# Last 512 queries in two halves, B's x loads behind the read of x's staging tile, six VectorE score banks in groups 3, 7 and 11

## Chip, cores, metric

One core of a Trainium2 chip runs the whole program. The metric is device time in microseconds of an execution. A run is called fast or slow by its state; slow runs are left out of every comparison. Ratios are computed as the mean time of one kernel's fast runs over the mean of the other's fast runs of the same rounds, so they are not quite the ratio of the medians quoted beside them.

## The reference

Two attention blocks over 2048 positions of width 448, 16 heads of 28, bf16. A has one key and value head that all query heads share, and full softmax over all 2048 keys. B looks back over 8 positions, two apart.

```python
def _A_ref(x, wq, wk, wv, wo):
    q = (x @ wq).reshape(B, S, H, Dh).transpose(0, 2, 1, 3)
    k = x @ wk; v = x @ wv                         # one head
    p = softmax(einsum("bhqd,bkd->bhqk", q, k) * Dh ** -0.5)
    return einsum("bhqk,bkd->bhqd", p, v) ... @ wo
def _B_ref(x, wqkv, wo):                           # window 8, dilation 2
    ...
return concatenate([a, b], axis=-1)
```

## The kernel before

A Python list scheduler lays out the order of all instructions on PE (TensorE), ACT (ScalarE), DVE (VectorE), POOL (GpSimd) and SP (SyncE) when the program is built, from estimated durations (below, `pr` is an operation's priority, lower first, and `rel` the earliest time for it in the list's own clock, in us); on the chip each engine runs its list in that fixed order. So a changed estimate, priority or dependence can reorder everything after it.

A's scores: a *quad* is 512 queries x 4 heads, 16 quads in all (group q below is quad q). Each quad has 64 score banks of 128 keys x 512 queries. ScalarE exponentiates three or two banks at a time; VectorE takes one of the three in some rounds.

```python
SLOTS = ((0, 1, 2), (3, 4))      # PSUM banks of the two score slots
PVBANK = 5; XBANKS = (6, 7)      # P.V sums; everything else
TAILB = (0, 1, 2, 4); WARM = 7
OFF_AT = {q: (0, 2, 5, 7) for q in range(1, 16)}             # rounds with a bank on VectorE
OFF_AT.update({q: (0, 2, 3, 5, 7, 8) for q in (5, 9, 13)})
```

The loads. x of A's first 512 rows goes to a staging tile (`xst`), the other chunks and B's x come by DMA transposes, all from one queue in the order of `pr`; A's chunks 1 to 3 (`pr=-20 + c`) wait for the staging tile, B's x (`pr=-16 + c`) doesn't wait.

```python
for c in range(1, NCH):      # A's chunks 1 to 3 wait for the staging tile
    ... e.dma_start(out=g.xT_A[...], transpose=True), R=["xst"], W=[("xT", c, t)], pr=-20 + c)
for c in range(NCH):         # B's x: no wait
    ... e.dma_start(out=g.xT_B[...], transpose=True), W=[("xT_B", c, t)], pr=-16 + c)
a("sp", ...  B's q and k weights ..., pr=-16.5, rel=4)
a("gp", ...  B's V weights (wqv) ..., pr=-7)
# ... wo_B, wo4 ..., pr=2
a("sp", ... e.dma_start(out=g.v_dram[0:PAD, :], in_=g.Vst[0:PAD, 0, :]),   # zero rows before V
  R=[("Vst", 0)], W=[("vd", -1)], dsem="i_vz", land=2.5, pr=3, rel=4)
```

B's V of each block of 128 rows is copied by VectorE from PSUM to `Vst[:, k % 2]` and stored to a scratch in HBM. The zero rows are stored *from* `Vst[:, 0]` too, so the first V copy has to wait until that store has read them.

The end of the last quad, cut:

```python
for hf in range(2 if last else 1):       # evacuation of P.V in halves, all after the last P.V
    ... transpose, reciprocal, tensor_tensor, transpose
for s4 in range(4):                      # four blocks of 128 queries
    u = Use(..., (TAILB[s4],), late=True) if last else Use(..., XBANKS)
    ... four output matmuls, one copy (VectorE, or ScalarE if last and s4 is odd), one store
```

Of the kernel before, what the change touches and what calls it, by code (L numbers as in the profile page):

```python
# [29 lines left out]
XBANKS = (6, 7)  # L30
TAILB = (0, 1, 2, 4)
WARM = 7
QT = 27.0
# [5 lines left out]
OFF_AT = {q: (0, 2, 5, 7) for q in range(1, 16)}  # L39
OFF_AT.update({q: (0, 2, 3, 5, 7, 8) for q in (5, 9, 13)})  # L40
LATE = 2
# [52 lines left out]
class Sched:  # L94
# [49 lines left out]
    def run(self, engines):  # L144
# [44 lines left out]
        while left:  # L189
# [77 lines left out]
            if e == "pe":  # L267
                if o.use is not None and o.use.spare and o.alone and area(T) < (self.WANT if limit is None or T + o.dur + 0.18 <= limit + self.EPS else self.LOW):
                    o.fill = 1
                    o.dur += 0.18  # L270
                    o.dense += 512 - o.use.spare
                elif (o.full and area(T) < (self.FULL[o.full] if T + 0.22 * o.full + 0.2 <= H + self.EPS else self.LOW)
                      and all(d.start is not None and d.end + self.lat(d) <= T for d in o.opt)):
                    o.deps.update(o.opt)
                    o.dur = 0.22 * o.full
                    o.tiled = False
                    o.dense = 512 * o.full
                elif o.fill is not None:
                    o.full = 0
                    o.fill = max(0, min(0 if waiting else 2, round((self.WANT - area(T)) * self.WIN / 512 + 0.3)))  # L280
                    if T > 14 and area(T) > self.LOW:
                        o.fill = max(0, min(o.fill, int((H - 0.12 - self.MODE - T - o.dur + self.EPS) / 0.22)))
                    o.dur += 0.22 * o.fill
                    o.dense += 512 * o.fill
                if o.tiled and not mode:
                    o.dur += self.MODE
                mode = o.tiled
                if o.dense:
                    recent.append((T + o.dur, o.dense))
                    del recent[:-120]  # L290
# [108 lines left out]
class Gen:  # L399
# [185 lines left out]
    def loads(self):  # L585
# [20 lines left out]
        for c in range(NCH):  # L606
            for t in range(4):
                a("sp", 1.05, one(lambda e, c=c, t=t: e.dma_start(
                    out=g.xT_B[:, t, 512 * c:512 * c + 512], in_=g.B_x[0, 512 * c:512 * c + 512, XB0[t]:XB0[t] + 128],
                    transpose=True)), W=[("xT_B", c, t)], dsem=f"i_xb{c}.{t}", land=4.5, pr=-16 + c)  # L610
        a("sp", 1.2, lambda e: [
# [113 lines left out]
    def a_q(self, sc, first=False):  # L725
# [3 lines left out]
        for t in range(4):  # L729
# [16 lines left out]
            else:  # L746
# [11 lines left out]
              R=["qadd"], W=[("qT", par, t)], use=u, pr=pr if first else -1)  # L758

    def a_loop(self):  # L760
        g, a = self, self.s.add
        units = [(sc, t, tb, j) for sc in range(4) for t in range(4) for tb in range(16) for j in range(4)]
        assert len(units) == NU
        g.last_exp, g.pvs, g.evacs = {}, {}, []
        quads = {(sc, t): [[] for _ in range(4)] for sc in range(4) for t in range(4)}
        dqs = {k: [[] for _ in range(4)] for k in quads}
# [5 lines left out]
        while pos < NU:  # L772
# [9 lines left out]
            def qk(e, us=us, b0=b0, box=[]):  # L782
                for _ in range(box[0].fill):
                    e.matmul(g.bank(b0), g.warm[:, 0:128], g.warm[:, :], start=True, stop=True)
                for i, (sc, t, tb, j) in enumerate(us):
                    if box[0].full:
                        r = e.matmul(g.bank(b0 + i), g.kz[:, j, 128 * tb:128 * tb + 128], g.qT[:, sc % 2, t, :], start=True, stop=True)  # L787
                        continue
                    r = e.matmul(g.bank(b0 + i), g.kT[32 * j:32 * j + 32, 128 * tb:128 * tb + 128],  # L789
                                 g.qT[32 * j:32 * j + 32, sc % 2, t, :], start=True, stop=True, tile_position=(32 * j, 0))  # L790
                return r
            box = []
            o = a("pe", 0.315, lambda e, qk=qk, box=box: qk(e, box=box), R=[("kT", tb // 4) for (_, _, tb, _) in us] + [("qT", sc % 2, t) for (sc, t, _, _) in us],
                  W=[("ring", slot)], pr=-50)
            box.append(o)
            o.ring = o.tiled = True
            o.full = len(us) if len(us) > 1 else 0
            o.opt = {x for (_, _, tb, _) in us for x in g.kz_ops[tb // 4]}
            o.fill = 0
# [10 lines left out]
            for i in range(na):  # L810
                g.last_exp[b0 + i] = x
                quads[us[i][:2]][us[i][3]].append((us[i], ("expT", n % ERING), g.expT[:, n % ERING, 512 * i:512 * i + 512], 0))
            if off:
# [4 lines left out]
            while late and late[0][0] <= n // 2:  # L818
                for x in late.pop(0)[1]:
                    qd = x[0][:2]  # L820
                    g.nq[qd] = g.nq.get(qd, 0) + 1
# [9 lines left out]
            for u in us:  # L831
                js = quads[u[:2]]
                while all(js):
                    g.pv_group([x.pop(0) for x in js])
                if u[2:] == (15, 3):
                    left = [x.pop(0) for x in js if x]
# [3 lines left out]
    def pv_group(self, grp):  # L840
        g, a = self, self.s.add
        qd = grp[0][0][:2]
        all_pv = g.pvs.setdefault(qd, [])
        box = []

        def pv(e):
            for (_, _, tb, j), _, src, w in grp:
                order = [o.seq for o, js in all_pv if j in js]
                first, last = box[0].seq == min(order), box[0].seq == max(order)
                x = e.matmul(g.bank(PVBANK, p0=32 * j, p1=32 * j + 32), g.v_aug[:, w, tb, :], src,  # L850
                             start=first, stop=last, tile_position=(0, 32 * j))
            return x
        o = a("pe", 0.315, pv, R=sorted({y[1] for y in grp}) + sorted(
            {(k, y[3], y[0][2] // 4) for k in ("v_aug", "v_aug1") for y in grp}), pr=-40, dense=700)
        o.tiled = o.pv = True
# [5 lines left out]
        g.npv[qd] = g.npv.get(qd, 0) + len(grp)  # L861
        if g.npv[qd] == 64:
            g.a_quad_end(*qd)

    def offload(self, n, us):

        g = self
        if n % 2 or us[0][:2] != us[-1][:2]:
            return 0
        if us[0][:2] != g.quad:  # L870
            g.quad, g.round = us[0][:2], n // 2
        return int(n // 2 - g.round in OFF_AT.get(4 * us[0][0] + us[0][1], ()))

# [26 lines left out]

    def a_quad_end(self, sc, t):
        g, a = self, self.s.add
        end = 12.0 + QT * (4 * sc + t + 1)
        last = sc == 3 and t == 3
        evacs = []
        hv = 2 if last else 1
        for hf in range(hv):
            w, b = 512 // hv, 16 // hv
            cs, bs = slice(w * hf, w * hf + w), slice(b * hf, b * hf + b)
            keys = [hf] if last else [0, 1]  # L910
            kk = lambda n: [(n, t % 2, x) for x in keys]
            p0 = -30 if last else -1
            o = a("dve", t_dve_ps(w), lambda e, cs=cs: e.transpose(out=g.PV_T[:, t % 2, cs], in_=g.bank(PVBANK)[:, cs]),  # L913
                  W=kk("PV"), pr=-30)
            o.deps.update(x for x, _ in g.pvs[sc, t])
            evacs.append(o)
            pt = g.PV_T[:, t % 2, :].rearrange("p (b e) -> p b e", e=32)
            a("dve", 0.25, lambda e, pt=pt, bs=bs: e.reciprocal(out=g.rden[:, t % 2, bs], in_=pt[:, bs, DH]),
              R=kk("PV"), W=kk("rden"), pr=p0)
            a("dve", t_dve_1x(w), lambda e, pt=pt, bs=bs: e.tensor_tensor(  # L920
                out=g.oN[:, bs, :], in0=pt[:, bs, :], in1=g.rden[:, t % 2, bs].unsqueeze(2).to_broadcast([128, b, 32]), op=ALU.mult),
              R=kk("PV") + kk("rden"), W=[("oN", x) for x in keys], pr=p0)
            a("dve", 0.12 + 1.04e-3 * w, lambda e, cs=cs: e.transpose(
                out=g.oTn[:, t, cs], in_=g.oN[:, :, :].rearrange("p b e -> p (b e)")[:, cs]),
              R=[("oN", x) for x in keys], W=[("oTn", t, x) for x in keys], pr=p0)
        g.evacs = evacs
        pr = end + 20
        if t < 3:
            return
        for s4 in range(4):  # L930
            blk = 4 * sc + s4
            if last:
                u = Use(f"F{sc}.{s4}", (TAILB[s4],), late=True)
            else:
                u = Use(f"F{sc}.{s4}", XBANKS)
            for tt in range(4):
                o = a("pe", t_mm(D), lambda e, u=u, s4=s4, tt=tt: e.matmul(  # L937
                    g.bank(u.bank, D), g.oTn[:, tt, 128 * s4:128 * s4 + 128], g.wo4[:, tt, :], start=tt == 0, stop=tt == 3),
                  R=[("oTn", tt, s4 // 2), "wo4"], W=[u], use=u, pr=pr + s4 + tt if not last else -30 + tt, dense=448)
                if last and tt == 0:  # L940
                    o.deps.add(g.last_exp[TAILB[s4]])
            ob = blk % 4
# [63 lines left out]
    def b_logits(self, k):  # L1006
# [4 lines left out]
        for t in range(4):  # L1011
# [9 lines left out]
            if k == 0:  # L1021
                op.deps.update(g.s.rd.get("xst", ()))
        u = Use(f"L{k}", XBANKS, spare=128)
# [114 lines left out]
```

## Time and profile before

| | before |
|---|---|
| median | 461.12 us, 461.11 over the six runs of the comparison |
| first exponential starts / last ends | 11.29 / 451.72 us |
| span of the profile | 459.19 us |
| head, stream, tail | 11.29, 440.43, 7.47 us |
| TensorE clock | 1.000 |

"Stream" is from the start of ScalarE's first score exponential to the end of the last, "tail" from there to the end of the span. In a row of a profile stand the start and the duration in us (chain, timeline), or busy us and mean ns of one (groups); what follows in brackets or behind the last bar is the idle time of the engine before it and what ended it. PEld is PE's weight load.

### The profile page before, as it was taken

What the parts mean: (1) busy time and instruction counts of PE and PEld (TensorE: products, weight loads), DVE (VectorE), ACT (ScalarE), POOL (GpSimd) and SP (SyncE); (2) the same over time, 40 slices, a digit from 0 to 9 for tenths busy, and PEclk for the clock granted to TensorE, in tenths of its full rate; (3) what the DMA queues carried; (4) which work ended last, traced back from release to release, by engine and by line L of the source; (5) the groups of instructions that cost most, each with busy time, mean ns of one, the idle gap of its engine ahead of it and who ended that gap; (6) DMA issues with size and microseconds to landing.
All of it is one profiled execution on the core that took longest, in us unless ns stands there. A gap on an engine that the chain in (4) does not pass through costs nothing.

```text
span 459.2 us, 8717 instructions
## 1 busy us (share of the span) xinstructions
PE 427.7 (93%) x3682; PEld 163.6 (36%) x3682; DVE 380.7 (83%) x622; ACT 444.9 (97%) x430; POOL 9.4 (2%) x29
## 2 busy tenths in 40 slices
PE   8999999999999989999899999899899998989997
PEld 3333232323533324234353342224244342325343
DVE  6556889988798898989688889998988969889883
ACT  3999999999999999999999999999999999999994
POOL 7000000000000000000000000000000000000000
PEclk9999999999999999999999999999999999999999
DMA  7774303002201002020220120002022221214001
GB/s 152 128 162 95 109 27 100 1 1 90 92 15 40 19 10 82 20 81 22 81 91 30 44 83 18 0 13 92 0 97 92 70 78 30 72 31 142 10 1 61
DMA packets 42102, 27.34 MB, mean 60 GB/s; under 512 B 17474, under 2 KB 41904, under 8 KB 42064
## 3 DMA queue, kind: packets, MB, share of 16 engines
q1 hardware_dynamic: 40464, 25.28, 19.6%
q0 software_dynamic: 304, 0.73, 0.6%
q10 hardware_dynamic: 1296, 0.79, 0.5%
q8 instruction: 29, 0.48, 0.4%
q14 instruction: 9, 0.07, 0.1%
HBM read 17.60 MB, written 5.52 MB: 50 GB/s over the span
## 4 chain that ended last, share of the span: by engine, by line
ACT 86%; PE 11%; DVE 1%; DMA 1%; issue 0%
ACT expT L806 85%; PE ps L789 2%; PE ps L1079 2%; PE ps L850 2%; PE ps L787 1%; DMA stage<-in_A_x_dram 1%; PE ps L978 1%; PE ps L1086 1%; PE ps L937 1%; ACT e_t L1054 0%; PE ps L654 0%; PE ps L738 0%; PE ps L1028 0%; PE ps L434 0%; PE ps L993 0%
## 5 line engine op out<-in xcount | busy, mean ns | idle before, releaser
L806 ACT ACTIVATE expT<-ps 128x1024 bf16<-128x1024 f32 (+1 forms) x410 | 438.8, 1209 | 2.1 <-PE ps L789 1.9
L789 PE MATMUL ps<-qT,kT 32*128 32x512 bf16 x824 | 122.3, 385 | 11.6 <-ACT expT L806 9.3
L850 PE MATMUL ps<-expT,v_aug 128*32 128x512 bf16 x958 | 94.8, 389 | 1.0 <-ACT expT L806 1.0
L787 PE MATMUL ps<-qT,kz 128*128 128x512 bf16 x200 | 59.6, 383 | 9.9 <-ACT expT L806 9.4
L789 PEld LDWEIGHTS ps<-qT,kT 32*128 32x128 bf16 x824 | 30.1, 91 | 91.7 <-ACT expT L806 68.4
L883 DVE TENSOR_SCALAR d_x<-ps 128x512 f32<-128x512 f32 x66 | 45.4, 688 | 17.9 <-PE ps L789 16.8
L850 PEld LDWEIGHTS ps<-expT,v_aug 128*32 128x32 bf16 x958 | 24.3, 93 | 62.0 <-issue 55.4
L1073 DVE TENSOR_TENSOR prod<-Vsh,a_n 128x896 bf16<-128x896 bf16 x64 | 37.5, 614 | 7.9 <-PE ps L1079 7.9
L1019 DVE TENSOR_TENSOR stage<-qTB,kTB 112x1024 bf16<-112x1024 bf16 x64 | 42.3, 674 | 1.8 <-PE ps L1028 1.7
L1079 PE MATMUL ps<-ident,prod 128*112 128x128 bf16 x512 | 41.8, 224 | 0.0
L894 DVE SCALAR_TENSOR_TENSOR d_u<-d_u,d_x 128x1024 f32<-128x1024 f32 x33 | 40.1, 1215 | 0.1
L896 DVE SCALAR_TENSOR_TENSOR dexp<-d_u,d_x 128x1024 int16<-128x1024 f32 x33 | 40.0, 1213 | 0.1
L892 DVE SCALAR_TENSOR_TENSOR d_u<-d_x 128x1024 f32<-128x1024 uint16 x33 | 39.9, 1209 | 0.2
L1079 PEld LDWEIGHTS ps<-ident,prod 128*112 128x112 bf16 x512 | 34.2, 130 | 14.7 <-issue 10.9
L978 PE MATMUL ps<-xT_B,wqkv 128*128 128x512 bf16 x128 | 38.9, 383 | 0.0
L787 PEld LDWEIGHTS ps<-qT,kz 128*128 128x128 bf16 x200 | 12.2, 97 | 31.1 <-ACT expT L806 28.9
L1028 PEld LDWEIGHTS ps<-ones,stage 112*128 112x128 bf16 x512 | 18.5, 96 | 7.8 <-issue 4.8
L1028 PE MATMUL ps<-ones,stage 112*128 112x4 bf16 x512 | 21.2, 167 | 0.0
L738 PE MATMUL ps<-xT_A,wq 128*128 128x512 bf16 x64 | 19.8, 384 | 0.1
L1086 PE MATMUL ps<-wo_B,oT 112*128 112x448 bf16 x64 | 18.1, 357 | 0.0
L993 PE MATMUL ps<-wqv,xT_B 128*128 128x448 bf16 x64 | 17.5, 356 | 0.0
L913 DVE STREAM_TRANSPOSE PV_T<-ps 128x512 f32<-128x512 f32 (+1 forms) x17 | 11.4, 676 | 6.7 <-PE ps L850 6.5
(103 smaller groups left out, 303.3 us busy)
## 6 DMA issues: line engine op xcount, KB each, us to landing
Vsh<-v_scratch SPq DMA_DIRECT2D x16, 896.0 KB, 4.6
v_scratch<-Vst SPq DMA_DIRECT2D x16, 112.0 KB, 1.7
out_dram<-outB SPq DMA_DIRECT2D x16, 112.0 KB, 1.7
out_dram<-outA SPq DMA_DIRECT2D x14, 112.0 KB, 1.7
wqkv<-in_B_wqkv_dram SPq DMA_DIRECT2D x1, 672.0 KB, 5.4
stage<-in_A_x_dram ACTq DMA_DIRECT2D x1, 448.0 KB, 4.0
wo_B<-in_B_wo_dram SPq DMA_DIRECT2D x4, 98.0 KB
wo<-in_A_wo_dram SPq DMA_DIRECT2D x4, 98.0 KB
```

The source lines that it names most:

```text
L787: r = e.matmul(g.bank(b0 + i), g.kz[:, j, 128 * tb:128 * tb + 128], g.qT[:, sc % 2, t, :], start=True, stop=True)
L789: r = e.matmul(g.bank(b0 + i), g.kT[32 * j:32 * j + 32, 128 * tb:128 * tb + 128], g.qT[32 * j:32 * j + 32, sc % 2, t, :], start=True, stop ...
L806: x = a("act", t_exp(w), lambda e, b0=b0, w=w, n=n: e.activation(g.expT[:, n % ERING, 0:w], g.ps[:, 512 * b0:512 * b0 + w], ACT.Exp, scale ...
L850: x = e.matmul(g.bank(PVBANK, p0=32 * j, p1=32 * j + 32), g.v_aug[:, w, tb, :], src, start=first, stop=last, tile_position=(0, 32 * j))
L883: o = a("dve", t_dve_ps(512), lambda e: e.tensor_scalar(out=xx[:, 512 * h:512 * h + 512], in0=g.bank(bank), scalar1=-128.0 * A2, scalar2=1 ...
L892: a("dve", t_dve_1x(1024), lambda e: e.scalar_tensor_tensor(out=u, in0=lo, scalar=EP * F, in1=lo, op0=ALU.add, op1=ALU.mult), R=di, W=["d_ ...
L894: a("dve", t_dve_1x(1024), lambda e: e.scalar_tensor_tensor(out=v, in0=u, scalar=EQ * F * F, in1=lo, op0=ALU.add, op1=ALU.mult), R=["d_u"] ...
L896: a("dve", t_dve_1x(1024), lambda e: e.scalar_tensor_tensor(out=out, in0=v, scalar=EL / F ** 3, in1=xx, op0=ALU.mult, op1=ALU.subtract), R ...
L978: a("pe", t_mm(512), lambda e, u=u, t=t, kt=kt, w=w: e.matmul(g.bank(u.bank), g.wqkv[:, kt, w * D + KC * t:w * D + KC * t + 128], g.xT_B[: ...
L1019: op = a("dve", t_dve_2x(1024), lambda e, t=t, qv=qv, kv=kv: e.tensor_tensor(out=g.prodT[0:KC, t, :, :], in0=qv, in1=kv, op=ALU.mult), R=R ...
L1028: r = e.matmul(g.bank(u.bank, 128).rearrange("p (h w) -> p h w", w=WIN)[:, 4 * t:4 * t + 4, w], g.prodT[0:KC, t, w, :], g.ones4[:, :], sta ...
L1079: a("pe", 0.056, lambda e, u=u, t=t, w=w: e.matmul(g.bank(u.bank, 128, 128 * t, p1=KC), g.prod2[:, w, KC * t:KC * t + KC], g.ident[:, :], ...
```

## The change

Its intent: split the last quad so that half of it is finished before the stream ends; keep B's transposes from going ahead of A's; let B's first products wait only for PE's reads of the staging tile; take VectorE's extra banks earlier.

```diff
-TAILB = (0, 1, 2, 4)
-WARM = 7
+TAILB = (4, 0)
+WARM = 9
-OFF_AT.update({q: (0, 2, 3, 5, 7, 8) for q in (5, 9, 13)})
+OFF_AT.update({q: (0, 2, 3, 5, 7, 8) for q in (3, 7, 11)})
+OFF_AT[15] = (0, 2, 3, 5)
@@ the scheduler's estimate after filler matmuls
-                if o.tiled and not mode:
+                if o.tiled and (not mode or o.fill):
@@ B's x loads
-                    transpose=True)), W=[("xT_B", c, t)], ...
+                    transpose=True)), R=["xst"], W=[("xT_B", c, t)], ...
@@ the last quad's units: 2 x 128 keys by 256 queries, first half of the queries first
+    def parts(self, u):
+        if u[:2] == (3, 3):
+            return [(2 * (u[2] % 8) + i, 256 * (u[2] // 8), 256) for i in range(2)]
+        return [(u[2], 0, 512)]
@@ scores and P.V: one matmul for each part; P.V sorted by parts
@@ evacuation and output of each half on its own (cut)
-        for s4 in range(4):
+        for s4 in range(4) if hf is None else (2 * hf, 2 * hf + 1):
@@ B's first products
-                op.deps.update(g.s.rd.get("xst", ()))
+                op.deps.update(o for o in g.s.rd.get("xst", ()) if o.eng == "pe")
```

## The prediction

> **What bounds the kernel now.** I read the page first: busy shares, the chain that ended last, the costliest groups. Then the chain in order of time, first over the whole span and then over its last 7 us; then the timeline of the head and of the last quad, a "quad" being the work for 512 queries by 4 heads.
>
> ```profile
> PE 427.7 (93%) x3682; PEld 163.6 (36%) x3682; DVE 380.7 (83%) x622; ACT 444.9 (97%) x430; POOL 9.4 (2%) x29
> ACT 86%; PE 11%; DVE 1%; DMA 1%; issue 0%
> L806 ACT ACTIVATE expT<-ps 128x1024 bf16<-128x1024 f32 (+1 forms) x410 | 438.8, 1209 | 2.1 <-PE ps L789 1.9
> L883 DVE TENSOR_SCALAR d_x<-ps 128x512 f32<-128x512 f32 x66 | 45.4, 688 | 17.9 <-PE ps L789 16.8
> ```
>
> The first line gives each engine's busy time, the second the chain's shares by engine. ScalarE's exponentials (line 806) are the chain. The first starts at 11.29 us and the last ends at 451.72, and in those 440.4 us ScalarE sat idle for 2 us at most. The span of 459.2 us is therefore a head of 11.3, a stream of 440.4 and a tail of 7.5. VectorE computes the exponential for 66 of the 1024 score banks (the last line's x66).
>
> The rows by form say what the stream is made of:
>
> ```profile
> L806 ACT ACTIVATE expT<-ps 128x1024 bf16<-128x1024 f32 x270 | 269.7, 1066 | 0.1
> L806 ACT ACTIVATE expT<-ps 128x1536 bf16<-128x1536 f32 x139 | 207.2, 1490 | 2.0 <-PE ps L789 1.9
> L1054 ACT ACTIVATE e_t<-lg 128x256 f32<-128x256 f32 x8 | 3.5, 434 | 0.0
> ```
>
> The fastest start-to-start distance in the timeline is 0.903 us for a 1024-wide one and 1.33 us for a 1536-wide one. Thus 270 x 0.903 + 139 x 1.33 = 428.7 us is the floor of the exponentials; the other exponentials of line 1054 add eight times about 0.3 = 2.5, the four small ones of the head 0.6 and the last 512-wide one 0.8. The remaining 7.8 us are many small waits for scores, spread evenly.
>
> The tail, as the chain has it:
>
> ```profile
> 452.03 0.36 PE ps L850 x4
> 452.38 0.02 issue
> 452.41 0.78 DVE PV_T L913 x2
> 453.19 0.24 DVE rden L918 x2
> 453.43 0.64 DVE oN L920 x2
> 454.07 0.36 DVE oTn L923
> 454.43 0.05 issue
> 454.48 0.75 PE ps L937 x3
> ...
> 455.78 0.60 DVE outA L947
> 456.39 0.59 DVE outB L1089
> ```
>
> After the last P.V matmuls, VectorE evacuates, normalises and transposes 512 queries, as two interleaved halves (x2); PE makes the output products, VectorE copies two blocks and then B's last block, and the store takes the rest, 456.98 to 459.2 = 2.2 us.
>
> **What the Trainium skill says.** (1) "ScalarE: Activation LUTs", section "What ACT_TABLE_LOAD costs": an ACTIVATE costs 0.833 ns per element plus a fixed part, neighbours overlapping. The trace agrees on the slope: (1.33 - 0.903)/512 = 0.834 ns. The time follows the width, so the number of banks is what counts. (2) "TensorE: Matmul & The Clock Gate", Part 3, "The mechanism": matmuls on different row tiles run together, they start in program order, and a weight load overlaps running matmuls only when its row group differs. The trace agrees as far as it goes: three tiled score matmuls end 0.39 us after the first starts, and the next kind starts after 0.32. It has no two on one row tile back to back. (3) Same page, Part 1: the array runs at half rate until a window of about 3.4 us was busy. The seven warm-up matmuls take 3.17 us, some 0.43 each, against 0.216 later; the clock record reads full speed from 7.07 us on. (4) "PSUM — Partial Sum Buffer", Terms, "Zero region": a group's first matmul clears flags in the whole bank. So the second half, in the same bank as the first, must wait for the first half's evacuation. The diff keeps that dependence; no trace here shows the flags.
>
> **The change part by part.**
>
> *Banks moved.* Twelve groups of four and three of six banks before; the same after: 12 x 4 + 3 x 6 = 66. Group 15 keeps four, all in its first half. ScalarE keeps 139, 270 and 1 exponentials, so the floor stays. Each pair of banks costs VectorE 2 x 0.69 + 3 x 1.21 = 5.0 us. Moving a pair from group 13 to 11 only helps if VectorE's backlog would otherwise drain sooner; B's last block already starts its products at 420 us, against a nominal 376 in the program, so VectorE is behind all along and its total before the last group is the same. I give it 0, with 0.6 either way for the reshuffled schedule.
>
> *Halves, in the tail.* Half of the last quad is evacuated some 13 us before the end. After the last P.V there remain one each of 0.39, 0.12, 0.32 and 0.36, with three gaps of about 0.06: 1.4 us against 2.02 (452.41 to 454.43), so 0.6 less. Then two output products remain in place of four, and one copy each on VectorE (0.60) and ScalarE (0.54) in parallel. The chain after the transposes becomes 0.05 + 0.6 for two products + 0.6 copy = 1.25, against 1.95 from 454.43 to 456.38: 0.7 less. B's last copy (0.59) goes as well if B has ended by then. The sum is 1.3 if B still comes last, 1.9 if not. I take 1.6.
>
> *Halves, on PE inside the last quad.* A 512-wide score matmul becomes two of 256 on the same row tile, issued unit by unit. An estimate from the 0.214 us that 512 columns stream for: three units start at 0, 0.107, 0.111, 0.218, 0.222 and 0.329 and end streaming at 0.436 against 0.222, so 0.21 more; two units 0.11 more. P.V, sorted by halves, stays within 0.1. In the last quad 45 score matmuls are tiled and 14 are full (those cost nothing extra), say nine ops of three and nine of two: 9 x 0.21 + 9 x 0.11 = 2.9 us; P.V 16 x 0.05 = 0.8. PE's slack there: 27.5 - 25.7 = 1.8 us idle, and eleven filler matmuls of which nine show, near 2.5. So PE about suffices in sum, but a score op has to fit into one exponential of the other slot. For three units that is about 0.18 to see ScalarE's end + 0.39 + 0.21 + 0.1 = 0.88 of 0.903. The schedule was laid out with 0.315 for a score op still, so wherever PE is dense the scores come late. I count a third of the 2.9 as stalls of ScalarE: +0.9 us.
>
> *Head.* Nine warm-ups at 0.427 end their issue at 1.25 + 3.84 = 5.09, and x's first transposes, which began at 4.88 with the landing of the stage tile, begin 0.2 later.
>
> ```profile
> 1.25 3.17 PE L646 MATMUL ps<-warm 128*128 128x512 bf16 x7 [1.25 <-DVE warm L543]
> 1.94 3.86 SPq L608 DMA_TRANSPOSE xT_B<-in_B_x_dram  x3
> 4.88 1.89 PE L654 MATMUL ps<-ident,stage 128*128 128x128 bf16 x16 [0.46 <-DMA stage<-in_A_x_dram]
> 5.84 16.61 SPq L603 DMA_TRANSPOSE xT_A<-in_A_x_dram  x12
> ```
>
> What follows is partly bound by the projection weights, so I expect about +0.1 at the first exponential. The new read of the stage tile keeps B's three early transposes behind the landing, so A's twelve start at about 4.9 rather than 5.84: 1 us early, for K chunks that the stream waits for only a little (0.5 us by 33 us). I count -0.1.
>
> *B's first products.* They waited for A's transposes too, the last of which landed at 24.2 us; but they began at 53.1. That wait cost nothing, and removing it, or loading B's x 3 us later, changes nothing.
>
> Sum: -1.6 + 0.9 + 0.1 - 0.1 + 0 = -0.7. The parameters look as though tuned together (banks, warm-ups), which argues for somewhat fewer stalls than I counted; I choose -0.9, so 460.2 us.
>
> **The rivals.** *PE becomes the bound of the last quad.* For: PE is busy 13.63 of 14 us from 438 to 452 already, with B's transposes and output in it; the score ops get longer. If two thirds of the 2.9 us stall ScalarE and B's last block is pushed wholly behind the last P.V (some 2.3 of transposes, 0.65, 0.9, 0.6 and 2.2 of store), the tail gains nothing: about 462. Against: fillers give way, and the first half's output products leave the tail. *VectorE frees early and B ends before the stream.* For: VectorE idles 5.2 us before the last evacuation, and group 15's banks end one or two rounds earlier. Then the tail is 1.9 shorter and stalls are near 0.3: about 459.3, with a lucky middle 458.8. *Nothing shows.* Tail and stalls cancel: 461.
>
> **Range and chances.** The terms run from -1.9 to about 0 in the tail, +0.2 to +2 in stalls, 0.6 either way in the middle, 0.3 in the head; together 458.8 to 461.7 us for eight in ten. Two per cent is 9.2 us, more than the whole tail, and the stream's floor does not change: within 2% 0.98, faster 0.01, slower 0.01.
>
> **What would show each step.** Exponentials by form 139, 270, 1 (if not, the floor moved). Last exponential's end: 451.7 before; 452 to 453 confirms stalls from the halved scores, and these should be waits for tiled score matmuls after 425 us. From the last P.V matmul's end to the span's end: 6.8 before, about 5 expected; the first half's evacuation near 440. First exponential within 0.3 of 11.29. B's first products still near 53. The prediction is wrong if score ops on halved columns take no longer than before, if B's last copy still comes 4 us after the last P.V, or if the stream's middle moves by over 1 us.

## The result

The changed kernel took 465.69 us in the median of six runs, against 461.11 of the kernel before: a ratio of fast runs of 1.0093 (95% interval 1.0077 to 1.011). That is slower, within 2%, and outside the range given. Five runs were fast, 464.65 to 466.54 us; the sixth, 471.91 us at a mean clock of 0.977, was slow and is left out (of the ratio; the median counts it, and that of the five fast runs is 465.51). Not one run had the full clock: the fast ones read 0.993 or 0.989, the profiled one of the kernel before 1.000.

The page of the changed kernel, busy shares, clock slices and the chain by engine:

```profile
PE 433.1 (94%) x3822; PEld 166.3 (36%) x3822; DVE 381.3 (82%) x623; ACT 444.9 (96%) x429; POOL 9.4 (2%) x29
PEclk9999889999999999999999999999999999999999
ACT 79%; PE 15%; DMA 3%; SPq 1%; DVE 1%; issue 0%; DVEq 0%
```

ScalarE's busy time is the same 444.9 us as before. The chain gives 7 points of ScalarE's share away, 4 of them to PE and 2 to DMA, and PE's clock dips in the fifth and sixth slice, 46 to 69 us, nowhere near the last quad.

Rows by form of the changed kernel:

```profile
L820 ACT ACTIVATE expT<-ps 128x1024 bf16<-128x1024 f32 x270 | 272.4, 1082 | 3.6 <-PE ps L803 3.2
L820 ACT ACTIVATE expT<-ps 128x1536 bf16<-128x1536 f32 x139 | 209.7, 1508 | 2.0 <-PE ps L803 1.7
```

The counts are 270 and 139, as forecast: the floor did not move. The idle time in front of the 1024-wide ones did, from 0.1 to 3.6 us.

| | before | after | difference |
|---|---|---|---|
| head | 11.29 | 10.88 | -0.41 |
| stream | 440.43 | 444.78 | +4.35 |
| tail | 7.47 | 7.03 | -0.44 |
| span | 459.19 | 462.69 | +3.50 |

To place the 4.35 us, I took every exponential's distance to the next and subtracted the floor of its width (0.903 or 1.33 us). Summed from 12 to 50 us this excess is 1.15 us more than before, from 50 to 70 us 3.85 more, and over all the rest 0.7 less. So most of it lies in 20 us, fourteen quads before the one that was split.

What happens there, from the view of V's staging tile in the changed kernel (what ended VectorE's wait before writing it, and who waited for that):

```profile
L1009 DVE CAST Vst<-ps x16: 596/619/625, 52.0 to 381.7; 128x448 bf16<-128x448 f32 x16
L627 SPq DMA_DIRECT2D v_scratch<-Vst x1: 393/393/393, 49.6 to 49.6; - x1
...
  DMA v_scratch<-Vst: 2.0, 1
...
  PE ps L990: 1.8, 1
```

and the same view before:

```profile
L997 DVE CAST Vst<-ps x16: 596/616/626, 51.9 to 378.9; 128x448 bf16<-128x448 f32 x16
L626 SPq DMA_DIRECT2D v_scratch<-Vst x1: 392/392/392, 46.5 to 46.5; - x1
...
  PE ps L993: 0.7, 2
```

The single store of V's zero rows left at 49.6 us, before at 46.5. VectorE's first V copy now waits 2.0 us for it, and PE waits 1.8 us for the bank which that copy should have emptied. Before, the copy waited for no DMA.

The windows around it, first before, then after (width of the window; busy us of PE, PEld, DVE, ACT, POOL with counts; granted clock; DMA share; GB/s):

```profile
50.60:53.00 2.40, 1.86 (x11) 0.41 (x11) 1.97 (x4) 2.40 (x4) 0.00 (x0) 1.00 0.00 0
53.00:56.00 3.00, 3.00 (x24) 1.07 (x23) 1.60 (x4) 3.00 (x4) 0.00 (x0) 1.00 0.26 71
56.00:60.00 4.00, 4.00 (x29) 1.05 (x29) 4.00 (x6) 4.00 (x5) 0.00 (x0) 1.00 0.60 205
```

```profile
50.60:53.00 2.40, 0.64 (x6) 0.13 (x6) 1.01 (x2) 1.80 (x2) 0.00 (x0) 1.00 0.09 25
53.00:56.00 3.00, 3.00 (x16) 0.61 (x14) 1.99 (x4) 1.87 (x2) 0.00 (x0) 0.62 0.28 76
56.00:60.00 4.00, 4.00 (x17) 0.86 (x14) 2.15 (x4) 2.65 (x3) 0.00 (x0) 0.50 0.59 201
```

During the wait PE works 0.64 of 2.40 us. Then its clock goes to half (the clock record: from 53.69 for 6.83 us). PE is now "busy" all the time and does 17 matmuls where it did 29, so ScalarE gets its scores late and works 2.65 of 4.00 us. The wait of 2 us is followed by a loss of 3.85 us: 1.39 of it before the clock fell, the rest after.

A second loss is smaller: the exponential after the one at 14.46 us starts 0.87 us late, as the last part of A's chunk 1 landed at 15.23 us, against 14.11 before, though it had been issued 1.17 us sooner (8.58 against 9.75).

Both point at one part of the diff, the new read `R=["xst"]` on B's x loads. Before, three of B's transposes filled the queue while the staging tile was still on its way. With the read they come after A's and after B's weights, and everything behind them in the queue, the store of the zero rows too, comes 3.1 us later.

The tail, chain in order of time, changed kernel:

```profile
455.97 0.33 PE ps L866 x8
456.30 0.29 PE ps L949
456.60 0.77 PE ps L1098 x4
457.37 0.05 issue
457.42 0.63 DVE outB L1101
458.04 0.05 issue
458.09 0.94 PE ps L949 x4
459.04 0.02 issue
459.06 0.04 DVE outA L959
```

From the end of the last P.V (456.30) to the end of the span it is 6.4 us, before 6.8. B's last copy is still there, now in the middle, and PE's output matmuls (line 949) wait behind it: two of the first half's blocks had not been put out yet, and one of them needed the bank that this copy empties.

### The profile page after: what moved, and what is told of

The parts are those of the page before. It is cut to its first block, busy times and chain, and to the rows that moved or that the text cites. A ratio compares the mean times of both kernels' runs of the same rounds, so it can differ in the third digit from the quotient of the medians.

```text
span 462.7 us, 9007 instructions
## 1 busy us (share of the span) xinstructions
PE 433.1 (94%) x3822; PEld 166.3 (36%) x3822; DVE 381.3 (82%) x623; ACT 444.9 (96%) x429; POOL 9.4 (2%) x29
## 4 chain that ended last, share of the span: by engine, by line
ACT 79%; PE 15%; DMA 3%; SPq 1%; DVE 1%; issue 0%; DVEq 0%
ACT expT L820 79%; PE ps L803 4%; PE ps L866 2%; PE ps L1091 2%; PE ps L990 2%; DMA xT_A<-in_A_x_dram 1%; PE ps L800 1%; DMA stage<-in_A_x_dram 1%; SPq L604 1%; PE ps L739 1%; PE ps L1098 1%; PE ps L949 1%; ACT e_t L1066 1%; DMA v_scratch<-Vst 1%; SPq L623 0%
## 5 line engine op out<-in xcount | busy, mean ns | idle before, releaser
L803 PE MATMUL ps<-qT,kT 32*128 32x512 bf16 (+1 forms) x894 | 126.6, 374 | 10.8 <-ACT expT L820 8.7
L866 PE MATMUL ps<-expT,v_aug 128*32 128x512 bf16 (+1 forms) x1018 | 95.3, 378 | 0.5 <-DVE v_aug L718 0.5
L803 PEld LDWEIGHTS ps<-qT,kT 32*128 32x128 bf16 x894 | 31.6, 91 | 94.8 <-ACT expT L820 70.0
L800 PE MATMUL ps<-qT,kz 128*128 128x512 bf16 (+1 forms) x194 | 54.2, 368 | 6.7 <-ACT expT L820 6.2
L1091 PE MATMUL ps<-ident,prod 128*112 128x128 bf16 x512 | 44.1, 225 | 0.0
L990 PE MATMUL ps<-xT_B,wqkv 128*128 128x512 bf16 x128 | 40.6, 395 | 1.8 <-DVE Vst L1009 1.8
L739 PE MATMUL ps<-xT_A,wq 128*128 128x512 bf16 x64 | 18.6, 383 | 0.0
L412 PE MATMUL ps<-warm 128*128 128x512 bf16 x54 | 18.1, 384 | 0.2 <-DVE lg L1054 0.2
```

The lines of the kernel that those rows point to most:

```text
L800: r = e.matmul(g.bank(b0 + i, nq, nq * k), g.kz[:, j, 128 * tb:128 * tb + 128], g.qT[:, sc % 2, t, q0:q0 + nq], start=True, stop=True)
L803: r = e.matmul(g.bank(b0 + i, nq, nq * k), g.kT[32 * j:32 * j + 32, 128 * tb:128 * tb + 128], g.qT[32 * j:32 * j + 32, sc % 2, t, q0:q0 + ...
L866: x = e.matmul(g.bank(PVBANK, nq, q0, p0=32 * j, p1=32 * j + 32), g.v_aug[:, w, tb, :], src[:, nq * k:nq * k + nq], start=first, stop=last ...
L990: a("pe", t_mm(512), lambda e, u=u, t=t, kt=kt, w=w: e.matmul(g.bank(u.bank), g.wqkv[:, kt, w * D + KC * t:w * D + KC * t + 128], g.xT_B[: ...
L1091: a("pe", 0.056, lambda e, u=u, t=t, w=w: e.matmul(g.bank(u.bank, 128, 128 * t, p1=KC), g.prod2[:, w, KC * t:KC * t + KC], g.ident[:, :], ...
```

## The experiments

Theory: the order of the loads costs the time, by the late store and by the late chunk, and PE's clock multiplies it. (That last part stays argued: no run has so long a pause at 51 us without the fall.) Rivals: the halved last quad, the moved banks, or one of the two order costs alone. For four of these kernels (the order alone, the early store, the late weights with early store, the late weights alone) the instruction lists of PE, DVE and ACT are identical to those of the kernel they are derived from; only DMA issues and, in two of them, one GpSimd copy beside them moved. Those four are clean tests. In the others the scheduler reshuffled the lists.

**1. The changed kernel without the order.**

```diff
-  transpose=True)), R=["xst"], W=[("xT_B", c, t)], ...
+  transpose=True)), W=[("xT_B", c, t)], ...
```

> The changed kernel without the one new read of x's staging tile in B's x loads, so that three of B's transposes again run before A's. Theory 'store queue': in the changed kernel the zero rows of V's scratch are stored 3.1 us later (49.56 against 46.46 us) because of the new order; VectorE's first V copy waits for that store until 51.99 us, PE then idles 1.8 us and its clock goes to half for 6.8 us. Without the order the store is issued near 46.5, that copy has no DMA wait, the clock stays at 1.000, and the time is 459.0 to 460.2 us. Rival 'halves': the halved last quad or the moved banks cost the time; then it stays at 464 to 466 us with a full clock or not. Rival 'late K chunk': only the 0.87 us stall at 14.5 us goes, and about 464 us remain.

Measured: 460.37 us against 460.70 before on the same chip, ratio 0.9992 (0.9977 to 1.0007); runs at a clock of 0.999 or 1.000. The store went out at 46.85 us, the first V copy waited 0.4 us for it rather than 2.0. Stream 439.99 us, tail 7.03. The time returns; the halves and the moved banks, which this kernel still has, are not what cost 4.6 us. The wait was said to vanish and kept 0.4 us, and the time is 0.2 above the stated range.

**2. The order alone, on the kernel before.**

```diff
-  transpose=True)), W=[("xT_B", c, t)], ...
+  transpose=True)), R=["xst"], W=[("xT_B", c, t)], ...
-  op.deps.update(g.s.rd.get("xst", ()))
+  op.deps.update(o for o in g.s.rd.get("xst", ()) if o.eng == "pe")
```

> The kernel before with only the order of B's loads (and the products' narrower wait). Theory 'store queue': the same late store, a DMA wait of about 2 us before VectorE's first V copy if the copy is due near 50 us there too, a clock below 1.000, and 463.5 to 467 us; the tail of 7.5 us stays. If that copy is due after 52 us in this schedule the wait is hidden and the time is 460.5 to 461.5; then the late store needs the rest of the change to bite. Rival 'halves': 461.1 as before.

Measured: 462.41 us against 460.70, ratio 1.0033 (1.0006 to 1.006). The store was late here too (49.80 us), but VectorE reaches its first V copy only at 54.3 us, so that wait is hidden, as the second branch said. In part that was luck: the copy came 2.4 us later than before because of the losses in the head, and at 51.9 us it would still have waited, for the last of the store's fifteen recorded landing signals came at 53.00. What cost time was the chunk: it landed at 16.15 us, ScalarE lost 2.03 us at 14.6 and 0.73 at 18.9 us, and in the profiled run the clock was at half from 16.27 for 3.41 us. So the second branch's 460.5 to 461.5 was missed; the head loss had been underrated. The four runs fall into two pairs: 460.67 and 461.49 us at clock 1.000, 463.32 and 463.42 us at 0.996. Same program, same chip: the pair with the lower clock is some 2.3 us slower. Only the run of 463.32 us has a trace, so how much of that is the fall, and how much a later chunk, is not shown.

**3. The changed kernel with the store of the zero rows early.**

```diff
-  W=[("vd", -1)], dsem="i_vz", land=2.5, pr=3, rel=4)
+  W=[("vd", -1)], dsem="i_vz", land=2.5, pr=-16.6, rel=4)
```

> The changed kernel with the store of V's zero rows moved ahead of the weights of B in the queue (about 21 us), everything else the same; B's loads keep the new order. Theory 'store queue': no DMA wait before the first V copy, the clock 1.000, 459.5 to 461 us. Rival 'late K chunk' or 'B's loads too late': the stall at 14.5 us (0.9) and perhaps a wait for B's x stay, and with the clock falling anyway 463 to 466 us.

Measured: 462.95 us against 460.70, ratio 1.0050 (1.0035 to 1.0065), clock 0.993 to 0.995 in all runs. The wait at 51 us is gone (store at 20.57 us, no DMA among the releasers). The chunk's last part landed at 15.72 us and, in the view of A's x loads, PE waited for it:

```profile
L604 SPq DMA_TRANSPOSE xT_A<-in_A_x_dram x12: 1227/1261/1311, 4.9 to 19.3; - x12
  PEld ps L668: 2.7, 2
  PE ps L668: 1.9, 2
```

ScalarE lost 1.73, 0.49 and 0.71 us between 14 and 20 us, and the clock was at half from 15.72 for 3.41 us. So the expectation of a single cost fell: the store explains about half, and the rival's 463 to 466 us was met but for 0.05 us, with twice the loss that it had named at 14.5 us.

**4. The halves alone**, with seven warm-ups, banks in 5, 9 and 13, the old order and the old estimate. Group 15 keeps its new rounds, all in the first half.

> The kernel before with the last 512 queries in two halves alone (with the narrower wait of the products, which costs nothing); banks in 5, 9 and 13, seven warm-ups and the old order. From the trace of the changed kernel, where six matmuls of 256 took 0.33 us to the next as three of 512 do, the halves should cost the stream nothing: last exponential's end within 0.7 us of 451.7, and the tail about 6.3 us against 7.5; 459.3 to 460.6 us. Rival 'halves': 463 us or more.

Measured: 462.05 us against 460.70, ratio 1.0029 (1.0012 to 1.0045), full clock. The stream is 440.83 us, 0.4 more than before, and its excess over the last 27 us is no larger than before (0.7 against 0.8). But the tail grew to 8.50 us: all 32 transposes of B's last block came after the last P.V (28 in one stretch, then 4), then its copy, products, copy and store. I had expected 6.3. So the halves cost the stream nothing and still, alone, lengthen the end, because other things moved behind B.

The matmuls themselves, from the timelines of the last quad, three banks of scores with the P.V after them. Before:

```profile
433.76 0.39 PE L789 MATMUL ps<-qT,kT 32*128 32x512 bf16 x3 [0.42 <-ACT expT L806]
434.08 0.40 PE L850 MATMUL ps<-expT,v_aug 128*32 128x512 bf16 x4
```

After, with six matmuls of 256 in place of three of 512:

```profile
431.64 0.40 PE L803 MATMUL ps<-qT,kT 32*128 32x256 bf16 x6 [0.30 <-ACT expT L820]
431.98 0.40 PE L866 MATMUL ps<-expT,v_aug 128*32 128x256 bf16 x8
```

0.32 us to the next kind before, 0.34 after; the median of such places in the whole trace is 0.32 (136 places) and 0.33 (8). The 0.21 us that I had added for each such group does not exist.

**5. The moved banks alone.**

```diff
-OFF_AT.update({q: (0, 2, 3, 5, 7, 8) for q in (5, 9, 13)})
+OFF_AT.update({q: (0, 2, 3, 5, 7, 8) for q in (3, 7, 11)})
```

> The kernel before with six VectorE banks in groups 3, 7 and 11 in place of 5, 9 and 13, nothing else. On record the prediction gave this 0, within 0.6 us. Theory 'groups shorten the end of B': B's last blocks come earlier, the tail of 7.5 us falls by 0.5 to 1.5 us, 459.6 to 460.6 beside a kernel before of about 460.7 to 461.1. Rival 'no effect': within 0.6 us of before.

Measured: 462.07 us against 460.73, ratio 1.0028 (1.0013 to 1.0043). Both expectations missed. The stream is 1.2 us shorter in the profile (439.23 us), the tail 2.1 longer (9.59): all 32 transposes of B's last block run after the last P.V, and the last copy follows at 457.28 us.

```profile
451.17 1.24 PE ps L937 x6
452.41 0.57 PE ps L1086 x3
452.98 1.06 PE ps L1079 x19
...
454.80 0.74 PE ps L1079 x13
...
457.28 0.62 DVE outB L1089
```

**6. Early store and B's V weights later**, on the changed kernel with its order.

```diff
   ... as in 3, and
-  W=["wqv"], dsem="i_wbv", land=5, pr=-7, ninc=2)
+  W=["wqv"], dsem="i_wbv", land=5, pr=-7, rel=20, ninc=2)
```

> The changed kernel with the early store of V's zero rows and, in addition, B's V weights loaded by GpSimd from 20 us on rather than at 8.9 us. Theory 'two costs of the order': with the order, A's second chunk of x lands only at 15.2 to 16.2 us (14.1 to 14.9 without it) among GpSimd's weight loads, ScalarE waits 0.9 to 2.9 us at 14.5 us and PE's clock may fall at 16 us. Without those weights in the way the chunk's last part lands before 13.5 us, the waits at 14 to 19 us go, the clock stays 1.000 up to the tail, and the time is 459.5 to 460.8. Rival 'the order itself delays the chunk': it lands after 15 us still and 462.5 to 463.5 us remain.

On the chip these loads were issued at 16.49 us instead of 8.93. Measured: 459.72 us against 460.73, ratio 0.9972 (0.9955 to 0.9988), clock 0.999 to 1.000. The chunk's last part landed at 12.56 us, and the same view as in 3 lists nobody who waited:

```profile
L604 SPq DMA_TRANSPOSE xT_A<-in_A_x_dram x12: 1222/1262/1263, 4.9 to 19.2; - x12
who waited for it (us, times):
busy tenths in 40 slices 0000000000000000000000000000000000000000
```

No exponential before 28 us started over 0.25 us late. With both costs taken away and the new order kept, the change is a gain of 0.3%. Part of that may be the late weights' own: no run has them on the kernel before.

**7. Banks back to 5, 9 and 13**, with halves, nine warm-ups, the new estimate and the old order.

> The changed kernel with the old order and with six banks in groups 5, 9 and 13 again (halves and nine warm-ups stay). Against the run without the order (460.37 us, tail 7.03) this shows what the moved groups give. The halves alone had a tail of 8.5 us, because B's last block was then 28 transposes behind the last P.V. Theory 'groups shorten the end of B': tail 8 to 9 us again and 461.5 to 462.5 us. Rival 'the warm-ups or the mode cost shorten it': tail near 7.0 and 460.4 us.

Measured: 461.69 us against 460.73, ratio 1.0021 (1.0006 to 1.0036), tail 8.51 us, as the theory said. Beside run 4, from which it differs in the warm-ups and the estimate alone (ratio 1.0029 there, tail 8.50), it also shows that these two give nothing that can be told from noise.

The tails of the profiles side by side:

| | banks in 5, 9, 13 | banks in 3, 7, 11 |
|---|---|---|
| not halved | 7.47 (before) | 9.59 (run 5) |
| halved | 8.50 (run 4), 8.51 (run 7) | 7.03 (run 1, changed kernel) |

Each alone lengthens the tail, together they shorten it. The tails go with how many of the 32 transposes of B's last block PE runs after the last P.V: none at 7.03 us, 10 at 7.47, all 32 at 8.50, 8.51 and 9.59. Why the scheduler puts them so in each case I did not follow further.

**8. The tail mended**, on run 1: the four last blocks have banks of their own, ScalarE takes two of the copies.

```diff
-TAILB = (4, 0)
+TAILB = (1, 2, 4, 0)
-        if t < 3:
+        if t < 3 or hf == 0:
             return
-        for s4 in range(4) if hf is None else (2 * hf, 2 * hf + 1):
+        for s4 in range(4):
-                u = Use(f"F{sc}.{s4}", (TAILB[s4 - 2],), late=True)
-                pr = -30
+                u = Use(f"F{sc}.{s4}", (TAILB[s4],), late=True)
+                pr = -30 if s4 > 1 else 500 + s4
```

> The run without the order, with the tail mended: in that run two of the first half's output products and both their VectorE copies still came after the last P.V, behind B's last copy, for want of a free bank. Here the four last blocks have banks of their own, and ScalarE, idle by then, takes two of the four copies. Expected tail 6.0 to 6.5 us against 7.03, 459.4 to 460.0 us. Rival: B's last copy sets the end, tail stays at 7.0.

Measured: 459.66 us against 460.73, ratio 0.9978 (0.9963 to 0.9993); tail 6.55 us, 0.05 above what was expected. In its profiled run the stream began early, at 10.92 us, and met the chunk not yet landed: 1.14 us lost at 14.6 us, without the new order. So the chunk's landing is a limit of its own. An early start alone is not enough: runs 4 and 7 began at 10.92 and 10.97 us and lost 0.39 and 0.21 us there, with the chunk at 14.91 and 14.84; here it landed at 15.71.

**9. Both repairs and the mended tail**, with the new order.

> The two repairs of the load order (early store of V's zero rows, B's V weights from 20 us) and the mended tail together, on the changed kernel. If the two gains are of different parts they add: stream as in the run with the repairs (439.7 us), tail as in the run with the mended tail (6.5): 459.0 to 459.4 us, 0.3 to 0.4% under the kernel before. Rival: an earlier start only meets the chunk's landing and the gain is lost: 459.7.

Measured over five rounds: 458.85 us against 460.84, ratio 0.9959 (0.9934 to 0.9984). Stream 439.68, tail 6.53: the two gains add. The interval is wide because one of its six runs took 460.70 us, and one of the eleven runs of the kernel before in this job 463.86 us at clock 0.996; without that one the ratio is 0.9965. So the old kernel too can lose clock; that run has no trace.

**10. Only the late weights, the store left late.**

> The changed kernel with only B's V weights loaded from 20 us on; the store of V's zero rows stays late (near 49.5 us). The fourth corner beside the changed kernel, the run with the early store, and the run with both repairs. Theory 'two costs of the order': no waits at 14 to 19 us; VectorE's first V copy waits for the store to about 52 us, ScalarE loses over 1 us at 51 us, PE's clock falls to half near 53 us for one or two stretches of 3.4 us; 461.5 to 464.5 us. Rival 'the late chunk alone was the cost': 459.7 us as with both repairs.

Measured: 466.57 us against 460.84, ratio 1.0113 (1.0084 to 1.0141), clock 0.989 in three runs and 0.996 in one. This is 2 us above the range that I gave; whether it is slower than the changed kernel, whose interval overlaps this one, is open. In the windows of this run:

```profile
50.60:53.00 2.40, 0.00 (x0) 0.00 (x0) 0.00 (x0) 0.88 (x1) 0.00 (x0) 1.00 0.15 41
53.00:56.00 3.00, 1.48 (x8) 0.35 (x9) 2.02 (x3) 0.26 (x1) 0.00 (x0) 0.61 0.12 38
56.00:60.00 4.00, 4.00 (x19) 0.78 (x16) 2.63 (x5) 3.24 (x3) 0.00 (x0) 0.50 0.70 229
60.00:64.00 4.00, 4.00 (x20) 0.87 (x18) 2.36 (x4) 2.05 (x2) 0.00 (x0) 0.51 0.00 0
```

And in the view of V's staging tile:

```profile
L627 SPq DMA_DIRECT2D v_scratch<-Vst x1: 392/392/392, 49.2 to 49.2; - x1
...
  DMA v_scratch<-Vst: 4.4, 1
...
  PE ps L990: 4.5, 1
```

VectorE's wait for the store was 4.4 us, not 2.0; its first V copy began at 53.43 us. Two things add up. The engines had lost nothing in the head, so VectorE was free at 49.06 us rather than 49.98. And the store itself, though issued 0.3 us earlier, let the copy go only 4.2 us after its issue, against 2.4 in the changed kernel; why is not shown. PE stood still through the whole first window, and the clock was at half for 10.24 us.

These four runs, with equal instruction lists on PE, DVE and ACT, form a square (ratio to the kernel before; median):

| | chunk late | chunk in time |
|---|---|---|
| store late | 1.0093; 465.69 (changed kernel) | 1.0113; 466.57 (run 10) |
| store early | 1.0050; 462.95 (run 3) | 0.9972; 459.72 (run 6) |

The chunk alone costs 3.2 us (462.95 - 459.72), the store alone 6.9 (466.57 - 459.72), both 6.0 (465.69 - 459.72). They do not add: 3.2 and 6.9 would be 10.1. In the traces VectorE's wait at the store is 2.4 us shorter when the head has been late: 0.9 because it arrives later, 1.4 because that store landed sooner. The rest is not traced to a cause, and that the store alone costs more than both is not clear of noise. The corners ran in four jobs, run 3 on another chip than runs 6 and 10; against their own runs of the kernel before the order is the same.

**11. Mended tail and late weights with the old order.**

> The mended tail with the old order of B's loads (three of B's transposes first) and B's V weights from 20 us on. Head waits at 14.6 us go (1.1 us in the run with the mended tail when its first exponential was early), 459.0 to 459.5 us. It should equal the other combination within 0.5 us if the order has no worth of its own.

Measured: 459.67 us against 460.84, ratio 0.9968 (0.9948 to 0.9988); no head wait over 0.25 us, tail 6.53. Higher than expected, and in median 0.8 us behind run 9 of the same job. Their intervals overlap, so which order is the better one stays open. Nor does the pair test the order alone: run 11 leaves the store where it was (46.64 us), and its first V copy waits 0.5 us for it.

## Why the prediction was wrong

*The step that failed* is the last of its parts, "That wait cost nothing, and removing it, or loading B's x 3 us later, changes nothing." The first half of it holds: B's products do not need what they no longer wait for. The second half looked only at those who read B's x. It did not look at what stands behind those loads in the same queue: the store of the zero rows, 3.1 us later, which VectorE's first V copy must wait for. The view of V's staging tile in the trace of before already had the store at 46.5 and the copy at 51.9 us; the store's last landing signal came at 49.65, so the slack was 2.2 us. The new order takes 3.1, and the change took from the other end too: VectorE was free for the copy at 49.98 us and PE's product for it ready at 50.22. With the chunk late in both, the late store cost 2.7 us (465.69 - 462.95).

A second expectation had failed beside it. B's first products, said to be "still near 53", began at 43.68 us, so the copy was due sooner. The narrower wait did not do that (55.47 in run 2, 53.22 in run 4); the nine warm-ups and the new estimate of filler matmuls did (43.21 in run 7, with the old order).

*Head, "1 us early, for K chunks that the stream waits for only a little".* The chunk was issued over 1 us earlier and landed over 1 us later, 15.23 against 14.11 us; in runs 2 and 3 it was 16.15 and 15.72. It shares the DMA engines with GpSimd's weight loads at that time, and when B's V weights went away it landed at 12.56. With the old order it landed at 14.11 to 15.71 us (before and runs 1, 4, 5, 7, 8), so the two orders overlap. The Trainium skill says in "DMA: Bandwidth & Descriptors", section "Issuing engines are not separate DMA queues", that DMAs from all issuing engines run on the same 16 DMA engines and interleave. Runs 3 and 6 agree: moving GpSimd's loads alone brought SyncE's transpose from 15.72 to 12.56 us. Why the mixture should be served more slowly in the new order is not shown. With the store early, the late chunk cost 3.2 us (run 3 against run 6).

*The clock.* The prediction named the half-rate state for the warm-up alone and gave no term to its return. When it returns can be worked out from the traces. In the four runs where it fell in the middle (the changed kernel, 2, 3, 10) every change of the clock lies a whole number of stretches of 3.41 us after it first became full: 47.79 us is 14 of them, 10.24 is 3. In the stretch just before the fall PE was busy 1.65, 1.63, 1.52 and 0.00 us, under half of it:

```profile
50.28:53.69 3.41, 1.65 (x15) 1.00 0.18 53
12.86:16.27 3.41, 1.63 (x9) 1.00 1.10 164
12.31:15.72 3.41, 1.52 (x7) 1.00 1.09 156
50.23:53.64 3.41, 0.00 (x0) 1.00 0.18 53
```

(PE alone; the changed kernel, then runs 2, 3 and 10.) Of all other such stretches at full clock in the thirteen traces that no fall followed, the least busy had 1.83 us (before, from 454.21), though some hold pauses of 1.1 to 1.2 us (1.18 in run 5); run 3 fell with a longest pause of 1.25. So here it was the share of a stretch, not the length of one pause. How long the clock then stays at half is not explained by that: in the changed kernel PE was busy all through both stretches.

*Halves on PE, "I count a third of the 2.9 as stalls": +0.9 us.* Measured 0, so one of the prediction's own signs of being wrong came true (halved columns take no longer): from 425 us to the end the excess is 0.4 us in the changed kernel and 0.8 before. The working assumed that a second matmul on the same row tile holds up the next tile. Its 0.18 us "to see ScalarE's end" is not in the trace either: of the score matmuls of before that waited for ScalarE, half started within 0.09 us of its end.

*Halves in the tail, -1.6 us.* Measured -0.44. The direction was right, the size was not: even the milder case ("if B still comes last", 1.3) left out that the first half's own output products would still lie in the tail, behind B. With that mended (run 8) the tail is 0.92 shorter than before.

*Banks moved, 0 with 0.6 either way.* Mis-sized: alone they cost 0.28%, and their sign depends on the halves.

*Head, 0.* Only seven of the nine warm-ups ran before x's first transposes, which began at 4.75 us (before 4.88); the other two ran at 6.18 and 6.62 us. The 0.2 us of delay did not come. The first exponential came 0.41 us earlier, which I do not credit to the change: where the clock became full between 5.8 and 6.1 us after the start, the first exponential was at 10.88 to 10.95 us with nine warm-ups and at 10.94 with seven (run 2), and where it became full near 7 us, at 11.25 and 11.29 with seven and 11.50 and 11.61 with nine. The four others, full at 3.92 to 5.48 us, lie at 10.67 to 10.97.

*What held:* the counts 139, 270 and 1; the stream as the thing that bounds; that the tail would get shorter; and that nothing here moves 2%.

## What to carry to other kernels

When a load moves in a queue, list what stands behind it in that queue and who waits for each of those, not only who reads the moved load; a store of a few rows that frees a buffer can be the one that bites. Where the engines run fixed lists such a wait passes on (here 2.0 us on VectorE became 1.8 us on PE), and when it reaches PE, ask what the pause does to its clock. And when several parts come together, read from the trace *where* the time went before judging the largest part: here it was fourteen quads away from it.

## What the Trainium skill lacked or had wrong

- "TensorE: Matmul & The Clock Gate", the table of goals: it advises no PE-idle gaps over about 3 us. As a limit that was too wide here: PE's clock went to half after stretches of 3.41 us whose longest pause was 1.8 us (changed kernel, run 2) and 1.25 us (run 3), with PE busy 0.44 to 0.49 of the stretch. The lengths of all four falls seen in the middle of a run are whole multiples of 3.41 us (3.41, 3.41, 6.83, 10.24), which fits the window that the page gives in Part 1.
- The same page, Part 3, "The mechanism": it tells of weight loads that wait where the row group is the same, but not what two short matmuls on one row tile do between matmuls of other tiles. Six of 256 columns, issued in pairs on three tiles, took 0.34 us to the next kind where three of 512 took 0.32.
- "DMA: Bandwidth & Descriptors", "Issuing engines are not separate DMA queues": agrees, but no page gives what a DMA transpose loses beside weight loads that GpSimd issued. Here the fourth transpose of a chunk took 6.65 us from issue to landing beside them (8.58 to 15.23) and 3.81 us without B's V weights (8.75 to 12.56).
